# An attention-and-MLP block in a hand-written instruction order: another order for the same instructions

## The chip, the cores and the metric

The kernel runs on one core of one Trainium2 chip. The metric is the device time of one execution in microseconds. Three executions of the kernel before are known (median 170.43 us), and one execution was profiled.

## The reference

For 2048 tokens of 512 features, all in bf16, two blocks follow each other. The first is linear attention with 32 heads of 16 features, on a layer-normalised input:

```python
def _A_ref(x, wqkv, wo):
    ...
    phi = lambda t: jnp.where(t > 0, t + 1, jnp.exp(t)) + 1e-6
    pq, pk = phi(q), phi(k)
    kv = jnp.einsum("bhsd,bhse->bhde", pk, v)
    z = jnp.einsum("bhsd->bhd", pk)
    num = jnp.einsum("bhqd,bhde->bhqe", pq, kv)
    den = jnp.einsum("bhqd,bhd->bhq", pq, z)[..., None] + 1e-6
    o = num / den
...
h = x + _A_ref(_layernorm(x, axis=-1), A_wqkv, A_wo)
h2 = h + _B_ref(_layernorm(h, axis=-1), B_w1, B_w2)
```

The second block, `_B_ref`, is a ReLU MLP of 512 to 1792 to 512 features.

## The kernel before, in words

The tokens are 16 tiles of 128; four tiles make a chunk, so there are four chunks of 512 tokens. All weights and activations stay on chip. PSUM is one tile, `bk`, of eight banks of 512 fp32 columns, and each matmul group names its bank by number.

No scheduler orders the instructions. `ORDER` (line 18) is a long string of words, and the last lines of the kernel function go through it and call one small function for each word. The numbers behind a name are its arguments, so `K.8.0` is the keys of tile 8 in bank 0, `Q.2.3.2` the queries of chunk 2, feature block 3, in bank 2, and `f.1.1.0.7` seven of the fourteen products of tile 1 in bank 1.

```python
for word in ORDER.split():
    name, *idx = word.split(".")
    ops[name](*map(int, idx))
```

Each engine carries out its own words in the order of the string; semaphores between engines follow from the data (a reader waits for the writer, and a writer of a bank or buffer for its last reader). So an instruction that must wait also holds up everything behind it on its engine. The engines are PE (TensorE, matmuls), DVE (VectorE), ACT (ScalarE), POOL (GpSimd, masks only) and SP (SyncE), which issues every DMA: loads, stores and transposing DMAs.

The words, in the order in which the stages come (the lines are those of the kernel before):

| words | engine, line | what they do |
|---|---|---|
| lx, lk, lq, lv, lo, l1, l2 | SP, L201 and L204 | loads of x and of the weights for keys, queries, values, output, MLP |
| warmf, warm | PE, L221 and L215 | matmuls of zeros, whose results nobody reads |
| S, A | DVE, L237 and L238 | statistics of a tile of x, and their mean and variance |
| R | ACT, L243 and L244 | 1 / standard deviation of one or more tiles |
| N | DVE, L262 | the normalised tile, into `h_nat` |
| T and E | PE L281, ACT L291 | transpose of a normalised tile (tiles 0 to 3) and the copy into `lnT` |
| X | SP, L302 | the same by a transposing DMA (tiles 4 to 15) |
| K | PE, L310 | four matmuls of 512 columns: the keys of a tile |
| F, U, M, D or W | ACT L328 and L331, DVE L335, L338 or L343 | phi of the keys: exp, relu, min(exp, 1), the sum of both; W takes relu and sum in one step |
| G | PE, L362 | four matmuls that add the tile's normalised input times phi(keys) into banks 4 to 7 |
| za, zf, z, zc, zh | DVE, PE | the sum of phi(keys) over all tokens |
| Q, qF, qU, qM, qD or qW | PE L318, ACT, DVE | the queries of a chunk and phi of them, two feature blocks at a time |
| gA, kv, kx, m, mA | ACT, PE, DVE | the state: values' weights times G, masked by head, times wo, into `m_sb` |
| dn, dnl, dnx | PE L459, ACT L465, ACT L472 | the denominators of a chunk, and their reciprocals in two pieces of two tiles, into `wk_sb` (its weights are no longer needed) |
| dt | SP, L491 | transposing DMA of a tile's reciprocals into `rd`; for tiles 2 and 6 rt (PE) with rv (DVE) or re (ACT) does it |
| dm | DVE, L495 | phi(queries) times the reciprocals, into `pqs`, two feature blocks at a time |
| h, hD | PE L505, DVE L511 | four matmuls of `pqs` with the state, and the sum with x: the residual `h_nat` |
| s, a, r, n, x (or t and e) | DVE, ACT, DVE, SP L303 | the second normalisation and its transposes |
| p, pA or pD | PE L521, ACT L527 or DVE L532 | four matmuls with w1, and relu of two banks into `acts` |
| f, fo, fd | PE L541, DVE L549, SP L556 | fourteen matmuls with w2, the last sum, the store |

The words of different stages are interleaved. In the first 30 us the keys of a tile follow as soon as its transpose is there, and G follows phi of the keys. From about 39 us the state, the denominators and the queries of the later chunks come, h of chunk 0 follows at 50 us, and from 61 us p, h and f of different chunks alternate until the stores at the end.

Of the kernel before, what the change touches and what calls it, by code (L numbers as in the profile page):

```python
# [28 lines left out]
qU.0.2.2 lo.0.2 z.3.1.14 z.2.1.14 G.15 z.1.1.14 z.0.1.14 qD.0.2.2 zc gA.0.2 gA.2.2 Q.1.0.2 zh dn.0.1 Q.1.1.3
dnl.0 kv.2.7 lo.2.2 kv.1.7 kv.3.7 dnx.0.2.2 qF.1.0.2 kv.0.7 l2.3.4 dnx.0.0.2 Q.1.2.0 l1.2.2 rt.2.6 kx qM.1.0.2  # L30
Q.1.3.1 qF.1.2.2 m.0.4 m.1.5 rv.2 Q.3.1.7 qW.1.0.2 m.3.6 Q.2.3.2 dt.3 qM.1.2.2 mA.0.2 qW.1.2.2 dt.0 dt.1 m.2.5
Q.2.1.4 dn.1.0 mA.2.2 dm.0.0.2 Q.2.2.1 dm.0.2.2 dnl.1 dnx.1.2.2 h.3.6 dnx.1.0.2 h.1.5 rt.6.3 hD.3 qF.2.2.2 dt.7
s.3 re.6 h.0.0 dt.4 qU.2.2.2 hD.1 dt.5 a.3 hD.0 s.1 s.0 a.1 qM.2.2.2 a.0 Q.3.0.6 Q.2.0.3 n.3 h.2.5 n.0 dm.1.0.2
Q.3.3.1 x.3 dm.1.2.2 qF.3.0.2 hD.2 n.1 s.2 Q.3.2.0 qU.2.0.2 qF.2.0.2 h.5.2 h.6.3 a.2 qU.3.0.2 qM.2.0.2 h.4.7 n.2
qF.3.2.2 x.0 qD.2.0.2 t.2.5 qD.2.2.2 hD.4 x.1 hD.6 h.7.4 dn.2.6 hD.5 hD.7 e.2 dnl.2 qM.3.0.2 p.0.0.5 dnx.2.2.2
p.0.13.7 p.0.1.6 p.0.8.2 p.0.9.3 dnx.2.0.2 qD.3.0.2 s.4 l2.7.3 p.0.11.4 pA.0.0.2 dt.11 l2.0.3 dt.9 dt.10 r.0.4
qM.3.2.2 qW.3.2.2 s.6 dt.8 p.0.12.6 s.7 pD.0.12.2 p.0.3.1 p.0.2.0 pA.0.8.2 dn.3.2 p.0.5.7 dnl.3 p.0.4.6 a.7
dm.2.0.2 pA.0.2.2 dnx.3.0.2 dnx.3.2.2 dm.2.2.2 pD.0.4.2 h.9.0 h.8.5 p.0.6.6 p.0.7.7 dt.13 dt.12 s.5 dt.14
# [553 lines left out]
```

## Time and profile before

| what | us |
|---|---|
| median of three executions (lowest to highest) | 170.43 (170.37 to 170.6) |
| span of the profiled execution, first to last instruction | 168.8 |
| PE busy (855 instructions recorded) | 163.1 |
| DVE busy (205) | 104.4 |
| ACT busy (97) | 65.1 |
| data moved by DMA | 15.49 MB |

The span is shorter than the time of an execution, since what lies before the first and after the last instruction isn't in it. Times within the profile count from the start of the span. "Idle before" and the name behind an arrow say how long an engine had nothing to do before an instruction, and what ended that. PE's matmuls overlap at their ends, so its busy time says little about holes; some matmul records are missing from a trace (here 16 of 867). A transposing DMA has two times: how long SP needed to issue it, and from its issue to its landing.

### The profile page before, as it was taken

Reading aid. Unit: us, or ns where it says so; the run is one execution under the profiler, and the core shown is the slowest. Engines: PE = TensorE matmul, PEld = TensorE weight load, DVE = VectorE, ACT = ScalarE, POOL = GpSimd, SP = SyncE. Lnnn points to the kernel's source line nnn. Section 1 sums busy time; section 2 is a strip of 40 time slices with the busy share of each in tenths; the row PEclk is TensorE's granted clock in tenths of the full one; section 3 lists DMA queues with packets and bytes.
Section 4 is the critical chain, followed back from the end, with each engine's and each line's share of the span. In section 5 each row is a group of like instructions: output and inputs, shape, how many; then the busy total and the mean of one; then the engine's idle time right before and its main releaser. Section 6 shows DMA issues by size and latency. Waiting matters only on the chain.

```text
span 168.8 us, 2286 instructions
## 1 busy us (share of the span) xinstructions
PE 163.1 (97%) x855; PEld 78.0 (46%) x871; DVE 104.4 (62%) x205; ACT 65.1 (39%) x97; POOL 4.8 (3%) x21
## 2 busy tenths in 40 slices
PE   7989999999999999999999999999999999999993
PEld 5344344445644454444444444444444444444553
DVE  3899998997668999699819879215102432050251
ACT  3698775875879947432000003004320420400000
POOL 7400000000000000000000000000000000000000
PEclk9999999999999999999999999999999999999999
DMA  4975575689533353534130015500320000002023
GB/s 112 352 245 97 97 66 124 176 270 378 174 64 65 77 138 87 134 62 95 37 62 0 31 31 122 126 4 0 62 93 0 31 0 4 0 0 93 0 65 94
DMA packets 30491, 15.49 MB, mean 92 GB/s; under 512 B 23184, under 2 KB 29328, under 8 KB 30480
## 3 DMA queue, kind: packets, MB, share of 16 engines
q1 hardware_dynamic: 30480, 15.34, 35.5%
q8 instruction: 7, 0.11, 0.3%
q14 instruction: 4, 0.03, 0.1%
HBM read 7.86 MB, written 2.10 MB: 59 GB/s over the span
## 4 chain that ended last, share of the span: by engine, by line
PE 85%; DVE 7%; DMA 4%; issue 1%; SPq 0%
PE bk L541 29%; PE bk L521 28%; PE bk L505 8%; PE bk L318 8%; PE bk L362 6%; PE bk L310 4%; DVE st L237 3%; DMA x_nat<-in_A_x_dram 2%; DMA lnT<-h_nat 2%; DVE h_nat L262 2%; PE bk L459 1%; DVE eb L335 1%; PE bk L403 1%; PE bk L415 1%; SPq L201 0%
## 5 line engine op out<-in xcount | busy, mean ns | idle before, releaser
L541 PE MATMUL bk<-w_sb,at 128*128 128x512 bf16 (+2 forms) x247 | 50.1, 355 | 0.3
L521 PE MATMUL bk<-lnT,w_sb 128*128 128x512 bf16 x219 | 50.0, 379 | 0.3
L527 ACT ACTIVATE at<-bk 128x1024 bf16<-128x1024 f32 x14 | 14.2, 1023 | 57.4 <-PE bk L521 57.4
L541 PEld LDWEIGHTS <-at 128*128 128x128 bf16 x252 | 23.6, 98 | 25.4 <-ACT at L527 0.3
L549 DVE SCALAR_TENSOR_TENSOR gT<-bk,rstd,h_nat 128x512 bf16<-128x512 f32 (+2 forms) x18 | 12.2, 689 | 35.7 <-PE bk L541 35.6
L521 PEld LDWEIGHTS <-w_sb 128*128 128x128 bf16 x224 | 21.8, 98 | 25.8
L532 DVE TENSOR_SCALAR at<-bk 128x1024 bf16<-128x1024 f32 x14 | 17.1, 1218 | 12.8 <-PE bk L521 12.6
L328 ACT ACTIVATE eb<-bk 128x1024 bf16<-128x1024 f32 (+1 forms) x18 | 16.6, 928 | 6.6 <-PE bk L310 4.8
L310 PE MATMUL bk<-wk_sb,lnT 128*128 128x512 bf16 x63 | 15.3, 380 | 0.4 <-ACT lnT L291 0.3
L505 PE MATMUL bk<-m_sb,pqs 128*128 128x512 bf16 x63 | 15.4, 380 | 0.1
L318 PE MATMUL bk<-lnT,wq_sb 128*128 128x512 bf16 x61 | 15.1, 379 | 0.1
L362 PE MATMUL bk<-at,h_nat 128*128 128x512 bf16 x55 | 13.5, 379 | 0.1
L331 ACT ACTIVATE rb<-bk 128x1024 bf16<-128x1024 f32 (+1 forms) x14 | 12.5, 904 | 0.3 <-PE bk L310 0.3
L511 DVE TENSOR_TENSOR h_nat<-bk,x_nat 128x512 bf16<-128x512 f32 x16 | 10.5, 680 | 2.9 <-PE bk L505 2.9
L237 DVE BATCH_NORM_STATS2 st<-x_nat 128x6 f32<-128x512 bf16 x16 | 10.8, 680 | 2.4 <-DMA x_nat<-in_A_x_dram 2.4
L239 DVE BATCH_NORM_STATS2 st<-h_nat 128x6 f32<-128x512 bf16 x16 | 10.7, 683 | 0.1
L310 PEld LDWEIGHTS <-lnT 128*128 128x128 bf16 x64 | 6.0, 98 | 8.4 <-ACT lnT L291 1.0
L362 PEld LDWEIGHTS <-h_nat 128*128 128x128 bf16 x64 | 6.2, 98 | 7.4 <-issue 0.2
L505 PEld LDWEIGHTS <-pqs 128*128 128x128 bf16 x64 | 5.9, 98 | 7.9 <-DVE pqs L495 1.8
L318 PEld LDWEIGHTS <-wq_sb 128*128 128x128 bf16 x64 | 5.9, 98 | 6.4
L472 ACT ACTIVATE wk_sb<-ld 128x1024 bf16<-128x1024 f32 x8 | 8.1, 1050 | 0.1
L335 DVE TENSOR_SCALAR eb<-eb 128x1024 bf16<-128x1024 bf16 (+1 forms) x18 | 6.8, 383 | 0.9 <-ACT eb L328 0.9
(63 smaller groups left out, 93.5 us busy)
## 6 DMA issues: line engine op xcount, KB each, us to landing
out_dram<-gT SPq DMA_DIRECT2D x15, 128.0 KB, 1.9
w_sb<-in_B_w_dram SPq DMA_DIRECT2D x2, 896.0 KB, 9.8
x_nat<-in_A_x_dram SPq DMA_DIRECT2D x2, 512.0 KB, 6.3
w_sb<-in_B_w_dram SPq DMA_DIRECT2D x2, 512.0 KB, 9.5
x_nat<-in_A_x_dram SPq DMA_DIRECT2D x3, 256.0 KB, 4.6
w_sb<-in_B_w_dram SPq DMA_DIRECT2D x2, 384.0 KB, 3.5
wk_sb<-in_A_wqkv_dram SPq DMA_DIRECT2D x2, 256.0 KB, 4.3
wq_sb<-in_A_wqkv_dram SPq DMA_DIRECT2D x2, 256.0 KB, 4.9
```

What stands on the lines that cost most here:

```text
L237: op_S = lambda t: nc.vector.bn_stats(out=st[:, t, :], in_=x_nat[:, t, :])
L310: nc.tensor.matmul(bk[:, b, :], lhsT=lnT[c][:, kd, j * P : (j + 1) * P], rhs=wk_sb[:, kd, :], start=(kd == 0), stop=(kd == KD - 1),)
L318: nc.tensor.matmul(bk[:, b, :], lhsT=wq_sb[:, kd, j * P : (j + 1) * P], rhs=lnT[c][:, kd, :], start=(kd == 0), stop=(kd == KD - 1),)
L328: nc.scalar.activation(out=buf(eb, kind, i, n), in_=bank(at_bank[kind, i], n), func=ACT.Exp)
L331: nc.scalar.activation(out=buf(rb, kind, i, n), in_=bank(at_bank[kind, i], n), func=ACT.Relu)
L362: nc.tensor.matmul(bk[:, KD + kd, :], lhsT=ln_nat[:, t, kd * P : (kd + 1) * P], rhs=pk(t)[:, 0, :], start=(t == 0), stop=(t == NT - 1),)
L505: nc.tensor.matmul(bk[:, b, :], lhsT=pqs[:, (c * KD + jb) % NQ, j * P : (j + 1) * P], rhs=m_sb[:, jb, :], start=(jb == 0), stop=(jb == KD ...
L521: nc.tensor.matmul(bk[:, b, cols], lhsT=w1_sb[:, kd, f * P : (f + 1) * P], rhs=lnT[c][:, kd, cols], start=(kd == 0), stop=(kd == KD - 1),)
L527: nc.scalar.activation(out=acts[c % 2][:, f : f + n, :], in_=bank(at_bank["p", c, f], n), func=ACT.Relu)
L532: nc.vector.tensor_scalar(out=acts[c % 2][:, f : f + n, :], in0=bank(at_bank["p", c, f], n), scalar1=0.0, scalar2=None, op0=ALU.max,)
L541: nc.tensor.matmul(bk[:, b, 0 : w * P], lhsT=acts[c % 2][:, f, j * P : (j + 1) * P], rhs=w2_sb[:, f, k * P : (k + w) * P], start=(f == 0), ...
L549: nc.vector.scalar_tensor_tensor(out=o_t[:, t % NO, cols], in0=bk[:, at_bank["f", t, k], 0 : w * P], scalar=rstd2[:, t : t + 1], in1=h_nat ...
```

## The change

Only the string `ORDER` changes, and it becomes two lines shorter, so that each later line number is less by two. The instructions are the same in kind, number and size; their order on the engines and some bank numbers differ. The first lines show the kind of edit:

```diff
-const lx.0.1 lx.1.1 warmf.4.3 warm.1.3 S.0 table A.0 R.0.1 S.1 lx.2.2 lk.0.2 warm.1.3 N.0 A.1 S.2 R.1.1 lk.2.2
-lx.4.2 A.2 T.0.7 E.0 warm.1.3 S.3 R.2.1 K.0.1.0.2 lx.6.2 A.3 R.3.1 K.0.1.2.2 N.1 T.1.5 F.0.1 E.1 N.2 N.3 T.3.2
...
+lx.0.1 lx.1.1 lx.2.2 lk.0.2 lk.2.2 lx.4.2 lx.6.2 lx.8.4 lx.12.4 lq.0.2 const warmf.4.2 warm.1.5 S.0 A.0 table R.0.1
+S.1 N.0 A.1 S.2 A.2 T.0.3 R.1.1 E.0 R.2.1 S.3 A.3 N.1 N.2 R.3.1 N.3 warm.1.7 warm.1.0 K.0.3.0.2 K.0.3.2.2 T.1.1 E.1
...
```

What differs, from the front to the end:

- The first ten loads stand at the head of the string; SP's own order of them is as it was. The first transposes write separate banks (3, 1, 4, 7), where two of them shared bank 5. Tile 1's keys come in one piece ahead of those of tiles 3 and 2, where they came in two halves around tile 3's. E.1 and E.3 go ahead of F.0 on ACT, and E.2 behind U.0.
- On DVE the statistics S of tiles 9 and 8 go behind N.7 and N.6, and A.6 goes ahead of N.4. In the tiles that follow, phi of the keys often takes U before F, tile 13 comes ahead of 12 in S, and tiles 9 and 8 or 12 and 13 change places here and there. K.13 follows K.12 directly, where G.9 stood between.
- On SP the load lq.2.2 (before: after X.10) and lv.0.2 (before: after X.14) go ahead of X.12; l2.7.3 (before: after the x of chunk 0) and l2.0.3 (before: after dt.11) go ahead of dt.3.
- In the state: the two pieces of the first reciprocals, dnx.0.2 and dnx.0.0, follow each other on ACT; rt.2 and the products m stand in other places between the queries; for chunk 3, dnx.3.0 stands ahead of pA.0.2 on ACT, where it stood behind it.
- In the MLP: p, h and f take other orders among the tiles, h.9 comes later, the stores of a chunk go in another order, and tile 15's three pieces of 256, 128 and 128 columns come one after the other at the end, where one of 128 stood earlier.

Three places follow as the built programs have them, row by row (line, instruction, what it writes and reads, size, and how often in a row). The first is DVE, from the statistics of tile 7 to those of tile 8 (BN_STATS is S, BN_AGGR is A, TENSOR_SCALAR into `h_nat` is N, the other two are M and D). Before:

```order
L237 BN_STATS st<-x_nat 128x6
L262 TENSOR_SCALAR h_nat<-x_nat,mv,rstd 128x512
L338 TENSOR_TENSOR pk_lo<-rb,eb 128x512
L335 TENSOR_SCALAR eb<-eb 128x512
L238 BN_AGGR mv<-st 128x2 x2
L338 TENSOR_TENSOR at_94<-rb,eb 128x512
L237 BN_STATS st<-x_nat 128x6
L262 TENSOR_SCALAR h_nat<-x_nat,mv,rstd 128x512 x2
L237 BN_STATS st<-x_nat 128x6
```

And now, at the same place:

```order
L235 BN_STATS st<-x_nat 128x6
L236 BN_AGGR mv<-st 128x2
L260 TENSOR_SCALAR h_nat<-x_nat,mv,rstd 128x512
L336 TENSOR_TENSOR pk_lo<-rb,eb 128x512
L236 BN_AGGR mv<-st 128x2
L333 TENSOR_SCALAR eb<-eb 128x512
L336 TENSOR_TENSOR at_94<-rb,eb 128x512
L260 TENSOR_SCALAR h_nat<-x_nat,mv,rstd 128x512 x2
L235 BN_STATS st<-x_nat 128x6 x2
```

One of the two BN_AGGR moved ahead of N.4, and the BN_STATS of tile 9 moved behind the pair of normalisations N.7 and N.6.

The second place is ACT around the first reciprocals (gT is the state's first part, `ld` the logarithm of the denominators, `wk_sb` their reciprocals, `eb` the exp of a query pair, `m_sb` the state). Before:

```order
L395 ACTIVATE gT<-bk 128x1024 x2
L465 ACTIVATE ld<-bk,eps_74 128x128
L472 ACTIVATE wk_sb<-ld 128x1024
L328 ACTIVATE eb<-bk 128x1024
L472 ACTIVATE wk_sb<-ld 128x1024
L328 ACTIVATE eb<-bk 128x1024
L418 ACTIVATE m_sb<-bk 128x1024 x2
```

And now:

```order
L393 ACTIVATE gT<-bk 128x1024 x2
L463 ACTIVATE ld<-bk,eps_74 128x128
L470 ACTIVATE wk_sb<-ld 128x1024 x2
L326 ACTIVATE eb<-bk 128x1024 x2
L416 ACTIVATE m_sb<-bk 128x1024 x2
```

The exp of a query pair that stood between the two reciprocals now stands behind both.

The third place is SP from the last big loads on (`w_sb` is w1 or w2, `rd<-wk_sb` is dt, `lnT_81<-hn` is x of chunk 0). Before:

```order
L204 DMA w_sb<-in_B_w_dram 128x4x512
L204 DMA w_sb<-in_B_w_dram 128x2x1792
L491 DMA_TRANSPOSE rd<-wk_sb 128x4x128 x6
L303 DMA_TRANSPOSE lnT_81<-hn 128x4x128 x3
L204 DMA w_sb<-in_B_w_dram 128x3x512
L491 DMA_TRANSPOSE rd<-wk_sb 128x4x128
L204 DMA w_sb<-in_B_w_dram 128x3x512
L491 DMA_TRANSPOSE rd<-wk_sb 128x4x128 x7
```

And now:

```order
L202 DMA w_sb<-in_B_w_dram 128x4x512
L202 DMA w_sb<-in_B_w_dram 128x2x1792
L202 DMA w_sb<-in_B_w_dram 128x3x512 x2
L489 DMA_TRANSPOSE rd<-wk_sb 128x4x128 x6
L301 DMA_TRANSPOSE lnT_81<-hn 128x4x128 x3
L489 DMA_TRANSPOSE rd<-wk_sb 128x4x128 x8
```

The two loads of 3 x 512 columns moved from among the transposes of chunks 0 and 2 to the place ahead of all dt.

More of the change, by code (lines that the diff above doesn't have):

```diff
@@ L29 @@
[L29 to L38, printed above, removed]
@@ new lines @@
+Q.1.1.3 dnl.0 dnx.0.2.2 dnx.0.0.2 qF.1.0.2 rt.2.5 kx rv.2 qM.1.0.2 qW.1.0.2 Q.1.2.0 Q.1.3.1 m.3.6 m.0.4 m.1.5 Q.3.1.7
+qF.1.2.2 Q.2.3.2 dt.3 qM.1.2.2 qW.1.2.2 mA.0.2 dt.0 dt.1 m.2.5 Q.2.1.4 dn.1.0 mA.2.2 Q.2.2.1 dm.0.0.2 dm.0.2.2 h.3.5
+hD.3 s.3 dnl.1 dnx.1.2.2 rt.6.3 h.1.0 h.0.5 hD.1 dnx.1.0.2 dt.7 re.6 qU.2.2.2 qF.2.2.2 dt.4 dt.5 Q.3.0.6 Q.2.0.3 h.2.2
+Q.3.2.0 Q.3.3.1 a.3 hD.0 n.3 s.0 qM.2.2.2 s.1 a.0 a.1 n.0 dm.1.0.2 dm.1.2.2 qU.2.0.2 qF.2.0.2 qF.3.0.2 qU.3.0.2
+qF.3.2.2 hD.2 n.1 s.2 qM.2.0.2 a.2 n.2 h.5.3 h.4.2 h.6.6 t.2.5 h.7.4 x.3 x.0 x.1 qD.2.0.2 qD.2.2.2 dn.2.7 qM.3.2.2
@@ new lines @@
+qM.3.0.2 qW.3.2.2 hD.4 qD.3.0.2 hD.6 hD.7 hD.5 e.2 dnl.2 dnx.2.2.2 r.0.4 dnx.2.0.2 dt.11 dt.9 dt.8 dt.10 p.0.0.5
+p.0.13.7 p.0.8.0 dn.3.2 p.0.9.1 p.0.1.6 p.0.11.4 dnl.3 pA.0.8.2 pA.0.0.2 p.0.2.0 p.0.3.1 p.0.4.5 p.0.12.6 dnx.3.0.2
+pA.0.2.2 s.6 s.4 s.7 s.5 dm.2.2.2 a.7 dm.2.0.2 pD.0.12.2 p.0.6.0 p.0.10.3 p.0.7.1 a.5 pD.0.6.2 dnx.3.2.2 pA.0.10.2
+p.0.5.6 h.9.4 h.11.3 h.10.7 dt.14 dt.12 dt.15 dt.13 n.5 pD.0.4.2 n.7 hD.11 a.6 n.6 hD.9 s.11 dm.3.0.2 a.4 dm.3.2.2
+h.8.0 a.11 n.4 n.11 s.9 hD.8 s.8 f.0.5.0.7 f.2.2.0.7 h.12.6 h.15.4 h.14.3 f.0.5.7.7 f.1.0.0.7 h.13.1 x.4 hD.15 x.6 x.5
```

42 lines of the change are left out of this document (20 added, 22 removed).

## The prediction

> **What bounds the kernel now.** First the page: the span, and the chain that ended last by engine.
>
> ```profile
> span 168.8 us, 2286 instructions
> PE 85%; DVE 7%; DMA 4%; issue 1%; SPq 0%
> ```
>
> TensorE (PE) carries 85% of the chain. The rest is a head that waits for the first inputs, and a tail. The same chain in order of time (start, length, what) says where PE takes over, what a matmul costs, and where PE ends.
>
> ```profile
> 17.65 3.40 DMA lnT<-h_nat
> 21.10 1.04 PE bk L310 x4
> 129.81 10.14 PE bk L521 x47
> 166.18 0.35 DVE gT L549
> ```
>
> From 21.10 us to 166.1 us the chain lies on PE. A matmul of 512 columns takes 10.14 / 47 = 0.216 us. The last store's add starts at 166.18 and the span ends at 168.8, so the tail is 2.6 us. The matmuls are the same in number and size after the change. So only PE's idle time can change: I look for it by comparing where a row of the PE timeline starts with where the one before it must have ended (its start plus its count times 0.216). The ends that the profile shows overlap, so they don't serve.
>
> ```profile
> 12.13 1.02 PE L362 MATMUL bk<-pk_lo,h_nat 128*128 128x512 bf16 x4
> 19.94 1.03 PE L362 MATMUL bk<-at,h_nat 128*128 128x512 bf16 x4
> 21.10 1.04 PE L310 MATMUL bk<-wk_sb,lnT 128*128 128x512 bf16 x4
> 24.56 1.03 PE L310 MATMUL bk<-wk_sb,lnT 128*128 128x512 bf16 x3
> 49.54 0.81 PE L318 MATMUL bk<-lnT,wq_sb 128*128 128x512 bf16 x3
> 50.25 2.07 PE L505 MATMUL bk<-m_sb,pqs 128*128 128x512 bf16 x8
> 52.16 0.39 PE L281 MATMUL bk<-ident,wk_sb 128*128 128x128 bf16 x4
> 61.24 0.55 PE L459 MATMUL bk<-zhd,pqT 128*128 128x8 bf16 x16
> 61.64 1.67 PE L521 MATMUL bk<-lnT,w_sb 128*128 128x512 bf16 x7
> 70.24 1.46 PE L521 MATMUL bk<-lnT,w_sb 128*128 128x512 bf16 x6
> 71.62 2.07 PE L505 MATMUL bk<-m_sb,pqs 128*128 128x512 bf16 x8
> 73.53 0.81 PE L521 MATMUL bk<-lnT,w_sb 128*128 128x512 bf16 x3
> ```
>
> Three holes stand there. **K.8** (tile 8's keys) starts at 21.10 where G.4 ended at 19.94 + 0.86 = 20.80: 0.30 us. **h.3**, the first product of chunk 0 with the state: 49.54 + 0.65 = 50.19 against 50.25, and its eight matmuls take 52.16 - 50.25 = 1.91 instead of 1.73: 0.24 us in all. **h.9**: 70.24 + 1.30 = 71.54 against 71.62, and 73.53 - 71.62 = 1.91 instead of 1.73: 0.26 us. All three wait for transposing DMAs. The first shows it in the chain; for the others it is VectorE (DVE) that waits, before the multiplications (dm) that feed h:
>
> ```profile
> 49.50 1.29 DVE L495 TENSOR_TENSOR pqs<-pqT,rd 128x1024 bf16<-128x1024 bf16 x2 [1.02 <-DMA rd<-wk_sb]
> 70.88 1.29 DVE L495 TENSOR_TENSOR pqs<-pqT,rd 128x1024 bf16<-128x1024 bf16 x2 [1.61 <-DMA rd<-wk_sb]
> ```
>
> Up to G.0 at 12.13 PE has much idle time, but there it waits for D.0, the last DVE step on tile 0's keys. So the head counts by D.0 alone.
>
> **The change part by part.**
>
> *Head.* These DVE rows are S.7, N.4, D.0 and the pair A.7, A.6 that follows:
>
> ```profile
> 10.74 0.68 DVE L237 BATCH_NORM_STATS2 st<-x_nat 128x6 f32<-128x512 bf16 x1
> 11.35 0.40 DVE L262 TENSOR_SCALAR h_nat<-x_nat,mv,rstd 128x512 bf16<-128x512 bf16 x1
> 11.66 0.42 DVE L338 TENSOR_TENSOR pk_lo<-rb,eb 128x512 bf16<-128x512 bf16 x1
> 12.20 0.24 DVE L238 BATCH_NORM_AGGREGATE mv<-st 128x2 f32<-128x6 f32 x2
> ```
>
> A.6 now stands ahead of N.4 and so ahead of D.0. One of the pair is worth at most 0.12, half of its 0.24, and at least nothing; as DVE has no gap here I take **+0.10**. G.0 moves from 12.13 to 12.23. The other head moves end before that. K.1 in one piece ahead of K.3 costs nothing if its copy E.1 is early, and it now stands ahead of F.0. On ScalarE (ACT) E.2 goes behind U.0:
>
> ```profile
> 10.20 0.58 ACT L291 ACTIVATE lnT<-bk 128x512 bf16<-128x512 bf16 x1
> 10.68 0.59 ACT L331 ACTIVATE rb<-bk 128x512 bf16<-128x512 f32 x1
> ```
>
> They change places, so E.2 ends where U.0 ended, at 11.27, and K.2's four matmuls run from 11.32 to 12.18, just ahead of the new G.0. That is cover by a few hundredths; whatever it falls short, G.0 pays. U.0 starts half a microsecond sooner, which D.0 can't use, as it stands behind N.4.
>
> *K.8.* X.8 was issued at 17.65 and landed 3.40 later. SyncE's queue (SP) issues ten such transposes from 10.85 on, with gaps; one gap is before X.7, which waits for N.7, which stood behind S.9 on DVE:
>
> ```profile
> 12.73 0.69 DVE L237 BATCH_NORM_STATS2 st<-x_nat 128x6 f32<-128x512 bf16 x1
> 13.33 0.72 DVE L262 TENSOR_SCALAR h_nat<-x_nat,mv,rstd 128x512 bf16<-128x512 bf16 x2
> 10.85 14.66 SPq L302 DMA_TRANSPOSE lnT<-h_nat  x10
> 13.75 1.19 SPq L302 DMA_TRANSPOSE lnT<-h_nat  x1
> ```
>
> N.7 and N.6 now go ahead of S.9, so they start up to 13.33 - 12.73 = 0.60 sooner. X.7 is third in line: X.5 and X.4 occupy SP from 10.85 for two steps of 1.27 (3.81 / 3, the row of three transposes further down), so X.7 can start at 13.4, 0.35 sooner than 13.75, and X.8, three places on, near 17.35. Even with the same 3.40 it lands at 20.75, and K.8 is due at 20.80 + 0.10 = 20.90. The hole goes: **-0.30**. A later landing leaves part of it. What is late next is below.
>
> *K.12 and K.13.* Two 256 KB loads (the second half of the query weights, the first of the value weights) now stand ahead of X.12 and X.13 on SP, and K.13 directly behind K.12, ahead of G.9. K.12 moves with PE from 24.56 to about 24.38, and K.13 is due 0.86 later, at 25.24. These rows are, in this order: X.13's issue, its time from issue to landing, that of the twelve transposes of this line together, and that of the three loads of this size that SP issued between 25 and 31 us.
>
> ```profile
> 21.11 1.19 SPq L302 DMA_TRANSPOSE lnT<-h_nat  x1
> DMA to landing us min/median/max: 4.1/4.1/4.1
> DMA to landing us min/median/max: 2.4/2.5/4.1
> DMA to landing us min/median/max: 2.9/3.0/3.1
> ```
>
> X.8 at 17.35, two load issues, X.12: X.13 is issued near 21.1 as before. With 2.5 it lands at 23.6 and nothing waits; with the 4.1 that it took, at 25.2, on the very point. With the loads in its way as well it is later by up to 1.2: the second load, issued at 19.2, lands 3.0 later, at 22.2, and if X.12 (issued at 19.8, due to land at 22.3) must follow it whole, it lands a step of 1.27 after that, and X.13 after X.12. So the bounds are 0 and 1.2. I take **+0.10**, near the low end, since the median of the twelve is 2.5. By the Trainium skill ("DMA: Bandwidth & Descriptors", Queues, rings and completion order), SP's DMAs share one row of rings, and each DMA engine consumes its ring in order; so the loads' bytes would go first. By that rule this term is the first rival's 0.66 whenever X.13 is as late as before. Whether a transpose waits for the loads ahead of it no row above shows.
>
> K.12 writes a bank that F.8 must have read. U.8 and F.8 change places, with R.10 now ahead of both: 0 to 0.1, I take **+0.03**. Q.2.3 waits in the same way for a DVE step (W of a query pair) that now comes behind rv.2: **+0.05**, between 0 and 0.1.
>
> *h.3.* dt.3, dt.0, dt.1 are transposes of the reciprocals, which ACT writes in two pieces (L472), with F of a query pair between them:
>
> ```profile
> 42.35 1.06 ACT L472 ACTIVATE wk_sb<-ld 128x1024 bf16<-128x1024 f32 x1
> 43.31 1.01 ACT L328 ACTIVATE eb<-bk 128x1024 bf16<-128x1024 f32 x1
> 44.21 1.05 ACT L472 ACTIVATE wk_sb<-ld 128x1024 bf16<-128x1024 f32 x1
> ```
>
> Now the two follow each other, so the second ends 44.21 - 43.31 = 0.90 sooner, and dt.0 and dt.1, which wait for it, can be issued sooner by half of that or more (dt.3 is ahead of them on SP). dm waited 1.02 and PE lost only 0.24, so a quarter of a microsecond is enough: **-0.24**. Against it: the last two w2 loads, 768 KB, now stand in front of dt.3. But one of 256 KB that stood there is gone ahead, another no longer delays X.15 before them, and SP comes to all of them sooner. I let this end between -0.24 and +0.24, as much the other way.
>
> *h.9.* Between the transposes of chunk 2 stood one of those loads, and another shortly before:
>
> ```profile
> 63.30 1.69 SPq L491 DMA_TRANSPOSE rd<-wk_sb  x1
> 65.04 0.58 SPq L204 DMA_DIRECT2D w_sb<-in_B_w_dram  x1
> 65.73 3.81 SPq L491 DMA_TRANSPOSE rd<-wk_sb  x3
> ```
>
> Without it the three at 65.73 go at least 65.73 - 65.04 = 0.69 sooner, and h.9 now stands later in PE's order: **-0.26**. What is late next here is ACT: dnx.3.0 (1.05) now stands ahead of the evacuation pA.0.2 (about 1.02, as the row of L328 for the same size). dnx.3.0 overwrites what dt.8 reads, so it waits for dt.8's landing, and p.0.6 waits behind both. p.0.0 started at 61.64 and by the terms so far comes 0.26 sooner, at 61.38; ten products of four matmuls (8.64) and the 16 small ones of dn.3 (0.40, as 61.24 to 61.64) stand ahead of p.0.6: due 70.42. dt.8 is the third of four, the first issued at 63.30 - 0.26; with two steps of 1.27, or one of 1.69 and one of 1.27, it is issued at 65.6 to 66.0, lands 2.5 later, and 2.0 later pA.0.2 has ended: 70.1 to 70.5. Cost 0 to 0.1, I take **+0.10**.
>
> *The rest* (order of p and f, banks, stores, the split of tile 15) changes none of PE's work. Each of these groups writes a bank whose emptying was put before other groups of four or seven matmuls, 0.9 to 1.5 us, and that is the cover; where it is gone, an evacuation of about 1.0 (L328's row, for two banks) shows as a hole. The last add and store have the size they had: 0.
>
> Sum: 0.10 - 0.30 + 0.10 + 0.03 + 0.05 - 0.24 - 0.26 + 0.10 = -0.42. The sum is against the profiled execution: 168.8 becomes 168.4. The median of the runs, 170.43, stands 1.6 above that span; I keep that distance: **170.0 us**.
>
> **The rivals.** About 0.2% (0.34 us) is what a measurement of this kernel can tell from no change; the forecast lies just beyond it.
>
> *The loads delay the transposes.* X.12's and X.13's bytes come after the loads' bytes, half of the 1.2 above since part of them is through by then, and X.13 again takes 4.1: it lands at 25.9 and K.13 waits 0.66 in place of 0.10. The sum is +0.14: 170.55. For it: X.13 took 4.1 with only other transposes around. Against: most transposes take 2.5, and 1.6 us of cover is there. Chance 0.24, of which 0.03 for nearly the whole 1.2 and an end on the slower side. The Trainium skill's rule on the rings, above, is this rival carried through.
>
> *A gain stays out.* The transposes before h.3 or h.9 are late for another reason than their place in the order (they took up to 4.1 elsewhere), and 0.25 is not won: 170.25. Chance 0.15, within 0.2%.
>
> *ACT behind dt.8.* If dt.8, issued at 66.0, takes 3.4 rather than 2.5, dnx.3.0 and pA.0.2 end at 71.4 and PE waits 1.0 at p.0.6: -0.42 - 0.10 + 1.0 = +0.48, 170.9. It decides for slower from a landing of 3.3 us on. For it: the 3.40 of X.8. Against: the load that stood among these transposes is gone. Chance 0.13.
>
> **How the numbers follow.** The forecast has 0.48; it is the likeliest. The range goes down to 169.7, where the new waits (0.28 without the head) don't come, and up to 170.75: it leaves out the slower ends and little else. Faster 0.48, within 0.2% 0.36 (0.21 and 0.15), slower 0.16 (0.13 and 0.03).
>
> **What would show it.** In the profile after: K.8 without a hole near 20.9; G.0 at 12.2; K.13 at 25.2 to 25.4; the DMA waits of L495 on DVE (2.6 us together) mostly gone and L505 running eight matmuls in 1.73; p.0.6 near 70.4; the last add near 165.75. I am wrong if a wait of PE above 0.3 us stands anywhere after 21 us, at K.13 or p.0.6 above all, or if the last add isn't sooner than 166.18.

## The result, and the profile after

The changed kernel took 171.72 us (median of four, 171.15 to 171.79), the kernel before 170.4 in the same series: a ratio of 1.0071, 95% interval 1.0049 to 1.0093. It is slower by about 1.3 us where 0.42 less was forecast, and above the range. Two later series with twelve executions each gave 1.0015 (0.9997 to 1.0032) and 1.0032 (1.0010 to 1.0053): the sign is the same, the size varies, and the first of the two can't be told from no change. Four executions of later series, of 248 to 608 us, are left out of the ratios.

The page after, first the span and the chain:

```profile
span 169.4 us, 2300 instructions
PE 83%; DVE 6%; DMA 5%; ACT 2%; issue 1%; SPq 0%; DVEq 0%
```

The span grew by 0.6 us, and DMA has 5% of the chain where it had 4%. The chain in order of time shows at which place:

```profile
19.91 4.96 DMA lnT<-h_nat
24.92 1.90 PE bk L308 x8
...
49.88 0.88 PE bk L316 x4
50.76 0.86 PE bk L503 x4
...
64.96 9.52 PE bk L519 x44
74.47 3.45 PE bk L503 x16
```

The first row is X.12, which took 4.96 us to land; K.12 and K.13 (24.92) follow it. The load lv.0.2 is the row just ahead of X.12 on SP; it landed 4.85 us after its issue, at 24.21, and X.12 0.66 after that, at 24.87:

```profile
19.36 0.46 SPq L202 DMA_DIRECT2D wv_sb<-in_A_wqkv_dram  x1
```

The other rows answer to the holes of before: h.3 starts at 50.76, where the queries end (49.88 + 0.88), and h.9 at 74.47, where 44 matmuls of the groups p (9.52 / 44 = 0.216 each) end without a gap, p.0.6 among them. The PE timeline around K.8 and K.12:

```profile
20.08 1.03 PE L360 MATMUL bk<-at,h_nat 128*128 128x512 bf16 x4
20.94 1.03 PE L308 MATMUL bk<-wk_sb,lnT 128*128 128x512 bf16 x4
21.80 2.75 PE L360 MATMUL bk<-at,h_nat 128*128 128x512 bf16 x12
24.92 1.90 PE L308 MATMUL bk<-wk_sb,lnT 128*128 128x512 bf16 x8 [0.36 <-DMA lnT<-h_nat]
```

K.8 (20.94) follows G.4 without a hole. Before K.12 the twelve matmuls end at 21.80 + 2.59 = 24.39, and K.12 starts at 24.92: 0.53 us are lost. On DVE the wait for the reciprocals is 1.5 us in place of 2.6:

```profile
L493 DVE TENSOR_TENSOR pqs<-pqT,rd 128x1024 bf16<-128x1024 bf16 x8 | 5.3, 678 | 1.5 <-DMA rd<-wk_sb 1.5
```

So up to the last matmul the changed kernel is a little ahead: its last add starts at 166.09, against 166.18. But its span ends 0.6 later. These rows of the timeline are the last stores on SP (start, duration) and the last add on DVE:

```profile
163.78 0.33 SPq L554 DMA_DIRECT2D out_dram<-gT  x1
164.44 0.33 SPq L554 DMA_DIRECT2D out_dram<-gT  x1
165.04 1.50 SPq L554 DMA_DIRECT2D out_dram<-gT  x1
166.63 0.86 SPq L554 DMA_DIRECT2D out_dram<-gT  x2
166.09 0.35 DVE L547 SCALAR_TENSOR_TENSOR gT<-bk,rstd,h_nat 128x128 bf16<-128x128 f32 x1 [0.43 <-PE bk L539]
```

From the DMA view of 164.5 to 165.0 us, the fetch of instructions on queue q8 (packets, MB, share of 16 engines):

```profile
q8 instruction: 1, 0.02, 18.4%
```

The issue of the store of 256 columns takes 1.50 us instead of 0.33, and the two stores behind it start at 166.63 and 167.11; the last could have started at 166.44, when its add ended. In the same stretch one packet of 16 KB fetches PE's next instructions; it took 0.184 x 16 x 0.5 = 1.47 us, from 164.70 to 166.17. From the start of the last add to the end it takes 3.35 us, not 2.66. I call this the tail.

The profile before has the same kind of row earlier: an issue of 1.03 us at 163.52, and then two of 0.33 with nothing in front of them; its packet (DMA view of 162.5 to 163.0 us) ran from 162.86 for 0.166 x 16 x 0.5 = 1.33 us:

```profile
163.52 1.03 SPq L556 DMA_DIRECT2D out_dram<-gT  x1
165.91 0.33 SPq L556 DMA_DIRECT2D out_dram<-gT  x1
166.56 0.33 SPq L556 DMA_DIRECT2D out_dram<-gT  x1
```

```profile
q8 instruction: 1, 0.02, 16.6%
```

In all twenty profiles of this case, altered kernels included, one issue beside this last packet is longer than the others, and it ends 0.2 to 0.4 us after the packet does (here 166.54 against 166.17). In the profile before that is over long before the last add.

### The profile page after: what moved, and what is told of

Its sections match the earlier page's. It is cut to its first block, busy times and chain, and to the rows that moved or that the text cites. A ratio compares the mean times of both kernels' runs of the same rounds, so it can differ in the third digit from the quotient of the medians.

```text
span 169.4 us, 2300 instructions
## 1 busy us (share of the span) xinstructions
PE 163.2 (96%) x871; PEld 77.7 (46%) x871; DVE 104.6 (62%) x205; ACT 64.6 (38%) x97; POOL 4.8 (3%) x21
## 4 chain that ended last, share of the span: by engine, by line
PE 83%; DVE 6%; DMA 5%; ACT 2%; issue 1%; SPq 0%; DVEq 0%
PE bk L539 29%; PE bk L519 29%; PE bk L316 8%; PE bk L503 8%; PE bk L360 4%; PE bk L308 3%; DMA lnT<-h_nat 3%; DVE st L235 3%; DMA x_nat<-in_A_x_dram 2%; DVE h_nat L260 1%; PE bk L457 1%; ACT rb L329 1%; ACT eb L326 1%; DVE at L336 1%; DVE mv L236 1%
## 5 line engine op out<-in xcount | busy, mean ns | idle before, releaser
L519 PE MATMUL bk<-lnT,w_sb 128*128 128x512 bf16 x224 | 49.5, 379 | 0.0
L316 PE MATMUL bk<-lnT,wq_sb 128*128 128x512 bf16 x64 | 15.6, 379 | 0.0
L241 ACT ACTIVATE rstd<-mv,eps 128x2 f32<-128x2 f32 (+2 forms) x14 | 4.1, 296 | 22.9 <-DVE mv L238 16.9
```

The source lines that it names most:

```text
L316: nc.tensor.matmul(bk[:, b, :], lhsT=wq_sb[:, kd, j * P : (j + 1) * P], rhs=lnT[c][:, kd, :], start=(kd == 0), stop=(kd == KD - 1),)
L519: nc.tensor.matmul(bk[:, b, cols], lhsT=w1_sb[:, kd, f * P : (f + 1) * P], rhs=lnT[c][:, kd, cols], start=(kd == 0), stop=(kd == KD - 1),)
```

## The experiments

The theory after the two profiles: the two loads delay X.12 (the first rival of the prediction, one transpose earlier than it said), and the fetch, whose place depends on the number of PE's instructions, holds up the last stores. The rivals: X.12 is late by the fetch near 22 us alone; the tail comes from the new order of the stores.

### The changed kernel again, and three first edits

No edit:

> The changed kernel once more, unaltered, as the mark for the others. Both theories expect 1.004 to 1.009 of the kernel before and, in the profile, the two losses seen once: a hole of about 0.5 us at K.12 near 24.9 and 3.3 us from the start of the last add to the end of the span, against 2.6 before.

Measured: 170.41 against 170.09, ratio 1.0015 (0.9997 to 1.0032), less than the 1.004 that both theories expected. The hole at K.12 was 0.31, the tail 3.03.

An earlier last piece:

```diff
-f.12.0.0.7 f.12.0.7.7 f.8.2.0.7
+f.12.0.0.7 f.15.4.0.14.3.1 f.12.0.7.7 f.8.2.0.7
...
-fd.12 fd.10 fo.8
+fo.15.3.1 fd.12 fd.10 fd.15.3.1 fo.8
...
-fo.15.2.1 fd.15.2.1 f.15.4.0.14.3.1 fo.15.3.1 fd.15.3.1
+fo.15.2.1 fd.15.2.1
```

> The changed kernel with the last 128 columns of tile 15 computed earlier, ahead of the second half of tile 12 (in the kernel before such a piece also stood earlier), and their add and store earlier with them. Theory 1 (the block of PE's instructions, 16 KB, that is fetched at 164.70 in the changed kernel and at 162.86 in the kernel before holds up SP's stores): with 14 small matmuls gone from the end, the fetch comes near 163, the tail falls from 3.3 to 2.6 us, and the time by about 0.7. Theory 2 (the order of the big stores: three of 128 KB come in the last microseconds, and the fetch does nothing): the big stores stay where they are, so the tail falls by 0.2 at most.

Measured: 1.0070 (1.0043 to 1.0097), slower than the unaltered kernel beside it (171.26 against 170.41 us), with a tail of 2.98: the numbers of both theories missed. The fetch came at 163.57, in the midst of the big stores. The DVE timeline shows what that did:

```profile
164.25 0.75 DVE L547 SCALAR_TENSOR_TENSOR gT<-bk,rstd,h_nat 128x512 bf16<-128x512 f32 x1 [2.01 <-PE bk L539]
166.55 1.40 DVE L547 SCALAR_TENSOR_TENSOR gT<-bk,rstd,h_nat 128x512 bf16<-128x512 f32 x3 [1.55 <-DMA out_dram<-gT]
```

An add waited 1.55 us for the landing of an earlier store, whose buffer it overwrites. A store delayed there costs more than one at the end. The edit changed order and fetch together and so can't tell the theories apart.

The loads back:

```diff
-lq.2.2 lv.0.2 X.12 X.13
+X.12 X.13
...
-X.10 K.12.0
+X.10 lq.2.2 K.12.0
...
-X.15 X.14
+X.15 X.14 lv.0.2
```

> The changed kernel with the two loads lq.2.2 and lv.0.2 behind X.10 and X.14 again, as in the kernel before. Theory 1 (the loads' bytes go ahead of X.12's and push them into the instruction fetch at 22.3): X.12 lands within 3 us, the hole of 0.53 us at K.12 goes, and the last add comes about 0.5 sooner, the time by 0.4 to 0.5. Theory 2 (the fetch alone delays X.12, as it delayed X.13 in the kernel before): X.12 or X.13 still takes 4 us or more and a hole of 0.3 or more stays.

Measured: 1.0031 (1.0008 to 1.0053), so the 0.4 to 0.5 us of theory 1 didn't come (170.65 against 170.41). The PE timeline at K.12, and at h.3 (of the four matmuls at 48.94 one record is missing, as 16 of the 871 are in this trace, and in the first profile of the kernel before):

```profile
21.73 2.54 PE L360 MATMUL bk<-at,h_nat 128*128 128x512 bf16 x11
24.10 1.89 PE L308 MATMUL bk<-wk_sb,lnT 128*128 128x512 bf16 x7
...
48.94 1.02 PE L316 MATMUL bk<-lnT,wq_sb 128*128 128x512 bf16 x3
50.04 1.21 PE L503 MATMUL bk<-m_sb,pqs 128*128 128x512 bf16 x4
```

K.12 starts as the eleven matmuls end (21.73 + 2.38 = 24.11): the hole is gone, so the loads made it. X.12 still took 4.2 us, with a fetch at 21.0 while it was under way (2.4 in the kernel before, where the fetch came later and X.13 took 4.1). That fits a delay by the fetch too; without the loads it doesn't reach K.12. What I hadn't expected: h.3 starts at 50.04, 0.24 after the queries' end (48.94 + 0.86), and its four matmuls take 1.21 instead of 1.03: 0.4 us. With the two loads later on SP, the w2 loads behind them are later too, and dt.3 lands 5.2 us after its issue (3.2 in the changed kernel). What the change paid at K.12 it had won back at h.3.

The late piece in the kernel before:

```diff
-f.13.4.0.7 f.15.0.0.14.3.1 f.14.5.7.7
+f.13.4.0.7 f.14.5.7.7
...
-fd.10 fd.11 fo.15.3.1 fo.8
+fd.10 fd.11 fo.8
...
-fd.12 fo.13 fd.15.3.1 fo.15.0.2
+fd.12 fo.13 fo.15.0.2
...
-fo.15.2.1 fd.15.2.1
+fo.15.2.1 fd.15.2.1 f.15.3.0.14.3.1 fo.15.3.1 fd.15.3.1
```

> The kernel before with tile 15's pieces of 256, 128 and 128 columns one after the other at the end, as in the changed kernel; all else as before. Theory 1 (fetch): the fetch moves from 162.9 to 164.6 or so, the tail grows from 2.6 to about 3.3, the time by 0.5 to 0.8. Theory 2 (order of the big stores, which is untouched here): the tail grows by 0.2 at most, 1.000 to 1.002.

Measured: 1.0005 (0.9985 to 1.0025). The fetch did move to 164.77, but the tail was 2.70: a fetch among the last stores doesn't always cost something. Its row in the DMA view (164.5 to 165.0 us):

```profile
q8 instruction: 1, 0.02, 10.9%
```

This packet took 0.109 x 16 x 0.5 = 0.87 us, not 1.47, and was over at 165.65, before the last add. The long issue beside it (0.50 us) ended at 166.02, and the last store started right behind its add, which ended at 166.27.

### Loads and fetch taken apart

> The changed kernel a third time, unaltered, as the mark for the three below and to see how far its distance from the kernel before moves from one series to the next (so far 1.0071 and 1.0015). Expected: 1.001 to 1.007, a hole of 0.3 to 0.5 us at K.12, a tail of 3.0 to 3.4 us.

Measured: 170.94 against 170.13, 1.0032 (1.0010 to 1.0053); hole at K.12 0.14, less than expected, and tail 3.08.

```diff
-lq.2.2 lv.0.2 X.12 X.13
+X.12 X.13 lq.2.2 lv.0.2
```

> The changed kernel with lq.2.2 and lv.0.2 behind X.13 in place of ahead of X.12: SP waits there for N.11 anyway, from 22.4 to 23.4. Theory 1 (the loads' bytes go ahead of X.12's): X.12 lands no later than 23.5 and the hole at K.12 falls from 0.3 to 0.5 us to less than 0.1, while h.3 stays without a hole, as SP is free just as early; the time is 0.3 to 0.5 below the unaltered changed kernel. Rival (the place of the loads doesn't matter, the instruction fetch near 21 to 22 delays X.12 or X.13 by itself): a hole of 0.2 or more stays at K.12 or K.13. Second rival: X.11 now follows the loads and lands late, and the hole moves to K.11.

Measured: 170.50, 1.0031 (1.0008 to 1.0053). The hole was gone and h.3 had none, as the theory says; X.12 landed at 23.0. From G.0 to the last matmul it took 153.12, the shortest so far. But the tail was 3.08. The median lay 0.44 below the unaltered kernel's, while the two ratios (1.0031 and 1.0032) are the same: a gain in time is not shown.

```diff
-p.2.5.5 p.2.4.4 p.2.8.6 p.3.1.3 p.3.8.0
+p.2.5.5.0.2 p.2.5.5.1.2 p.2.4.4.0.2 p.2.4.4.1.2 p.2.8.6.0.2 p.2.8.6.1.2
+p.3.1.3.0.2 p.3.1.3.1.2 p.3.8.0.0.2 p.3.8.0.1.2
```

> The changed kernel with five groups p (2.5, 2.4, 2.8, 3.1, 3.8) each computed in two halves of 256 columns: 20 matmuls more, the same columns, so PE takes no longer, but its instruction numbers run 20 matmuls ahead and the last fetch comes 20 matmuls earlier. Theory 1 (the last fetch, 16 KB at 164.70 in the first profile, holds up the stores around it): the fetch comes near 162.2, between the stores of 161.6 and 163.8; no store's issue takes over 0.6 from 163.7 on, the tail is 2.6 to 2.8 in place of 3.0 to 3.4, and the time 0.3 to 0.6 below the unaltered changed kernel. Theory 2 (the order of the stores): the tail stays at 3.0 to 3.4, the time the same within 0.1.

Measured: 170.07, 0.9991 (0.9974 to 1.0007), which is 0.87 below the unaltered kernel beside it, with the same order of stores. The DMA view of 160.0 to 160.5 us, then from the timeline the store of 256 columns and the last add:

```profile
q8 instruction: 1, 0.02, 12.2%
```

```profile
164.65 0.33 SPq L554 DMA_DIRECT2D out_dram<-gT  x1
165.71 0.35 DVE L547 SCALAR_TENSOR_TENSOR gT<-bk,rstd,h_nat 128x128 bf16<-128x128 f32 x1 [0.43 <-PE bk L539]
```

The fetch came at 160.43, earlier than I had expected; the store that took 1.50 us takes 0.33 like every one after 163; and the span ended at 168.36, 2.65 after the last add began. The executions also scatter less: 169.5 to 170.7, against 169.8 to 171.8.

> Both edits together. If theory 1 holds in both, the gains add: 0.6 to 1.1 below the unaltered changed kernel, and 0.2 to 0.8 below the kernel before (0.995 to 0.999). If only the loads matter it is as the run with the loads alone, if only the fetch matters, as the run with the split groups.

Measured: 170.01, 0.9998 (0.9982 to 1.0013); no hole at K.12, tail 2.67. The gains didn't add in the time: with the fetch away, the loads are worth less than this measurement can tell. That the tail is the fetch's stands (two of two with it moved, at 2.65 and 2.67, and the same order of stores).

### Were the two holes of the kernel before there to win?

> The kernel before, unaltered, for a second profile of it. Theory A (the prediction's: the holes before h.3 and h.9, 0.24 and 0.26 us, belong to the order of the instructions): they are there again, with DVE's waits of 1.0 and 1.6 us at L495, and from the start of G.0 to the start of the last matmul it takes 153.7 to 153.9 us as in the first profile. Theory B (they came of that one execution): at least one of them is absent, and the stretch takes about 153.4, as in the run with the late piece, which had neither.

> The kernel before, unaltered, for a third profile. Theory A: both holes, 153.7 to 153.9 us from G.0 to the last matmul. Theory B: at least one absent, about 153.4. Under both the hole at K.8 of 0.3 to 0.4 us is there.

Measured: 170.03 and 169.79, with spans of 168.3 and 168.1 where the first profile had 168.8. The PE timeline of the first at K.8, h.3 and h.9:

```profile
19.86 1.03 PE L362 MATMUL bk<-at,h_nat 128*128 128x512 bf16 x4
21.08 1.04 PE L310 MATMUL bk<-wk_sb,lnT 128*128 128x512 bf16 x4 [0.20 <-DMA lnT<-h_nat]
...
49.31 1.02 PE L318 MATMUL bk<-lnT,wq_sb 128*128 128x512 bf16 x4
50.17 1.89 PE L505 MATMUL bk<-m_sb,pqs 128*128 128x512 bf16 x8
51.90 0.39 PE L281 MATMUL bk<-ident,wk_sb 128*128 128x128 bf16 x4
...
69.55 1.89 PE L521 MATMUL bk<-lnT,w_sb 128*128 128x512 bf16 x8
71.28 1.89 PE L505 MATMUL bk<-m_sb,pqs 128*128 128x512 bf16 x8
73.00 2.32 PE L521 MATMUL bk<-lnT,w_sb 128*128 128x512 bf16 x10
```

K.8 lost 21.08 - 20.72 = 0.36 (0.32 in the other). But h.3 starts at 50.17, where the queries end (49.31 + 0.86), and runs its eight matmuls in 1.73; h.9 likewise (69.55 + 1.73 = 71.28; 73.00 - 71.28 = 1.72). Both holes are absent in both, and the stretch from G.0 to the last matmul takes 153.33 and 153.34, not 153.79. Theory B holds: I had priced two holes of one execution.

The two edits that I had given 0.50 us, alone in the kernel before:

```diff
-dnx.0.2.2 qF.1.0.2 kv.0.7 l2.3.4 dnx.0.0.2
+dnx.0.2.2 dnx.0.0.2 qF.1.0.2 kv.0.7 l2.3.4
...
-Q.1.2.0 l1.2.2 rt.2.6
+Q.1.2.0 l1.2.2 l2.7.3 l2.0.3 rt.2.6
...
-l2.7.3
...
-l2.0.3
```

> The kernel before with the two edits alone that the prediction gave 0.50 us: the first reciprocals dnx.0.2 and dnx.0.0 one after the other on ACT, and the loads l2.7.3 and l2.0.3 ahead of dt.3. Theory A (the prediction's): neither hole, 0.3 to 0.5 us less, 0.997 to 0.998 of the kernel before. Theory B (the holes came of one execution): h.9 has no hole, but there is nothing to gain on most executions: 0.999 to 1.001. Theory C (the two loads now queue ahead of dt.3, and without lq.2.2 and lv.0.2 gone from SP's queue before them they make it late, as in the run with the loads back, whose h.3 had a hole of 0.40): a hole of 0.2 to 0.5 at h.3, 1.000 to 1.003.

Measured: 170.95, 1.0053 (1.0039 to 1.0068), slower by more than any theory had said. The PE timeline at h.3, and dt.3's time from issue to landing:

```profile
49.56 1.02 PE L318 MATMUL bk<-lnT,wq_sb 128*128 128x512 bf16 x4
51.01 2.07 PE L505 MATMUL bk<-m_sb,pqs 128*128 128x512 bf16 x8 [0.43 <-DVE pqs L495]
```

```profile
DMA to landing us min/median/max: 5.2/5.2/5.2
```

h.3 waits 51.01 - 50.42 = 0.59, and its matmuls lose another 0.16; 0.25 more is lost at the query group before it (at 47 us). It is theory C, with a larger price: dt.3 stands behind 768 KB of loads and lands 5.2 us after its issue, at 48.56 and 0.5 after the last of these loads (48.06), as it lands 0.5 after its last load in all three profiles of the kernel before (46.33 after 45.83 in the first). So these edits lose by themselves, and the early loads lq.2.2 and lv.0.2 are what made them harmless in the change, as the run with the loads back says too (0.4 lost at h.3).

### Where the slower executions lose

> The changed kernel, unaltered, for one more profile: its executions scatter from 169.75 to 171.8 and those profiled so far lie in the faster half. Theory 1 (the last fetch, which holds up the stores for as long as its packet takes, makes the scatter): in a profile above 171 us the excess stands in the tail, 3.5 us or more, with a packet of 1.5 us or more. Theory 2 (the arrival of the x loads at the front): the excess stands before G.0, with lx.2.2 or lx.4.2 landing 0.5 or more later than 5.5 and 7.8. Theory 3 (the loads ahead of X.12): it stands between G.0 and the last matmul, over 153.6.

> As the run before: one more profile of the changed kernel, read in the same three stretches (to G.0, to the last matmul, tail), with the same three theories.

> As the two before: one more profile of the changed kernel, read in the same three stretches, with the same three theories.

Measured: 170.77, 170.94 and 170.89. None of them exceeded 171 us, so the theories could only be read from smaller differences. All unaltered profiles in three stretches (G.0's start from the timeline; G.0 to the start of the last matmul; the tail; the packet from the DMA view):

| kernel, us | G.0 | G.0 to last matmul | tail | span | last packet |
|---|---|---|---|---|---|
| before, first profile | 12.13 | 153.79 | 2.66 | 168.8 | 1.32 |
| before, second | 12.06 | 153.33 | 2.67 | 168.3 | 0.97 |
| before, third | 11.81 | 153.34 | 2.68 | 168.1 | 1.10 |
| changed, first profile | 12.24 | 153.60 | 3.35 | 169.4 | 1.47 |
| changed, second | 11.76 | 153.33 | 3.03 | 168.4 | 1.36 |
| changed, third | 12.09 | 153.22 | 3.08 | 168.6 | 1.27 |
| changed, fourth (170.77) | 12.02 | 153.41 | 3.29 | 169.0 | 1.42 |
| changed, fifth (170.94) | 11.93 | 153.31 | 3.66 | 169.1 | 1.70 |
| changed, sixth (170.89) | 12.87 | 153.27 | 2.78 | 169.2 | 0.94 |

In the changed kernel the tail grows with the packet, though not strictly (1.36 has 3.03, 1.27 has 3.08): the shortest packet has the shortest tail, the longest the longest. The run with the late piece fits too (0.87 and 2.70). The fifth profile in rows, the fetch (164.0 to 164.5 us; 0.212 x 16 x 0.5 = 1.70 us), then a store's issue and the last add, 3.66 before the end:

```profile
q8 instruction: 1, 0.02, 21.2%
```

```profile
164.44 1.80 SPq L554 DMA_DIRECT2D out_dram<-gT  x1
165.49 0.35 DVE L547 SCALAR_TENSOR_TENSOR gT<-bk,rstd,h_nat 128x128 bf16<-128x128 f32 x1 [0.43 <-PE bk L539]
```

The sixth is late for another reason: the load lx.4.2 landed at 8.88 us instead of 7.3 to 8.1, and all of the front is later with it. So theories 1 and 2 both make scatter, the loads (theory 3) little. The means of six against three: +0.15 at G.0, -0.13 between, +0.53 in the tail. Against the second and third profile of the kernel before alone, the middle is level: the 0.34 that K.8 lost there is spent at K.12 (0.28 on average) and in a new hole of up to 0.1 near 15.5 us. The profiles come from several chips; the median of the kernel before differs by 0.15 us among them (169.98 to 170.13).

### A version without the causes

First the two edits together with A.6 behind D.0 again:

```diff
-N.5 S.7 A.6 N.4 D.0.1 A.7
+N.5 S.7 N.4 D.0.1 A.7 A.6
```

> The changed kernel with the two loads behind X.13 and the five split groups, and in addition A.6 behind D.0 on DVE again, as in the kernel before. Expected by the stretches of the profiles so far: G.0 0.08 us sooner after X.5's issue (1.28 in place of 1.36), no hole at K.12, tail 2.65: 0.1 below the run with both edits, 0.998 to 0.9995 of the kernel before. Rival (A.6 isn't on the path, R.6 or N.6 behind it is): no difference.

Measured: 170.06, 0.9999 (0.9987 to 1.0011). G.0 still came 1.36 after X.5's issue (1.27 to 1.30 in the kernel before), so A.6's return alone wins nothing; and this execution shows a hole at K.11, the second rival of the run with the loads in the gap:

```profile
25.66 1.03 PE L360 MATMUL bk<-at,h_nat 128*128 128x512 bf16 x4
26.98 1.25 PE L308 MATMUL bk<-wk_sb,lnT 128*128 128x512 bf16 x5 [0.29 <-DMA lnT<-h_nat]
```

X.11, behind both loads, landed at 26.93, and K.11 lost 26.98 - 26.52 = 0.46.

Then one load behind X.13, the other behind X.10, and E.2 ahead of U.0 (the split groups and A.6 stay):

```diff
-lq.2.2 lv.0.2 X.12 X.13
+X.12 X.13 lq.2.2
...
-X.10 K.12.0
+X.10 lv.0.2 K.12.0
...
-R.4.2 U.0.1 E.2
+R.4.2 E.2 U.0.1
```

> The changed kernel with the five split groups, lq.2.2 behind X.13 and lv.0.2 behind X.10 (no load ahead of a transpose that is due at once), A.6 behind D.0 and E.2 ahead of U.0 again. Expected: no hole at K.12 and none at K.11, K.2's matmuls 0.5 sooner, so that G.0 comes 1.28 after X.5's issue instead of 1.36, about 153.1 from G.0 to the last matmul, tail 2.65: 0.998 to 0.9995 of the kernel before. Rival (h.3 is late again, since lv.0.2 is one place later): a hole of 0.2 to 0.4 at h.3, 1.000 to 1.002.

Measured: 169.70 against 169.99, 0.9985 (0.9971 to 1.0000). No hole at K.12 or K.11, 0.12 at h.3, tail 2.67. But G.0 came 1.41 after X.5's issue, so the return of A.6 and E.2 together wins nothing at the front either. The last two runs:

> The last run's best kernel, unaltered, once more: 0.9975 to 1.0 of the kernel before. Its profile showed that K.2's matmuls still began only at 11.24, where U.0 had read bank 3, which K.0 and K.2 share.

> The same kernel with K.0 in bank 0 in place of 3, so that K.2, in bank 3, no longer waits for U.0's reading of K.0. Theory (the shared bank, not the place of E.2 or A.6, delayed K.2 and with it G.0): K.2 starts within 0.1 of the end of E.2, G.0 comes 1.26 to 1.30 after X.5's issue in place of 1.36 to 1.43, and the time is 0.1 below that of the run beside it. Rival: G.0 stays at 1.36 or more.

```diff
-K.0.3.0.2 K.0.3.2.2
+K.0.0.0.2 K.0.0.2.2
```

Measured: 0.9985 (0.9971 to 0.9998) for the first, as in the series before it: 0.25 us less than the kernel before, with an interval that ends just below 1, and less than the changed kernel by more. For K.0 in bank 0: 0.9985 (0.9971 to 1.0000). The timeline at K.2 and G.0, first of the changed kernel itself (first profile; the second row is D.0 on DVE), then of the last kernel with the shared bank (its first series), then of the one with the other bank:

```profile
11.37 1.04 PE L308 MATMUL bk<-wk_sb,lnT 128*128 128x512 bf16 x4 [0.46 <-ACT lnT L289]
11.73 0.42 DVE L336 TENSOR_TENSOR pk_lo<-rb,eb 128x512 bf16<-128x512 bf16 x1
12.24 1.03 PE L360 MATMUL bk<-pk_lo,h_nat 128*128 128x512 bf16 x4
```

```profile
11.24 1.02 PE L308 MATMUL bk<-wk_sb,lnT 128*128 128x512 bf16 x4 [0.46 <-ACT rb L329]
```

```profile
11.18 1.04 PE L308 MATMUL bk<-wk_sb,lnT 128*128 128x512 bf16 x4 [0.76 <-ACT lnT L289]
12.47 0.81 PE L360 MATMUL bk<-pk_lo,h_nat 128*128 128x512 bf16 x3 [0.25 <-DVE pk_lo L336]
```

In the changed kernel K.2 waits for E.2, which stands behind U.0 on ACT, and G.0 follows K.2 without a hole (11.37 + 0.86 = 12.23); it is so in all twelve profiles with E.2 in that place. D.0, which ended at 12.15, isn't what ends last, and that is why A.6's return won nothing. With E.2 ahead of U.0, K.2 waits for U.0 (rb), which must have read K.0 out of the bank that both share. Only with the other bank as well does K.2 wait for E.2 at its old place, and G.0 (12.47) for D.0 again, 1.28 after X.5's issue. So E.2's place made the front's 0.1 us in the change, and the shared bank kept it when E.2 went back. What the bank alone, or A.6 alone, would cost no run shows. Won back, the 0.1 us doesn't show in the time.

## Why the prediction was wrong

Between the two first profiles, which the sum was about, two terms account for the miss: K.12's wait (0.53 where 0.13 was said for it and the bank) and the tail (0.68 where 0 was said). With the waits at p.0.6 and Q.2.3 that didn't come (0.15), they turn -0.42 into +0.51; the spans differ by +0.60, and a new hole of 0.07 near 15.5 us is most of the rest. The prediction's own sign of being wrong, a wait of PE above 0.3 us after 21 us, was there at K.12. Its other one was not, as the last add came at 166.09. Over several profiles a third term fails, that of h.3 and h.9.

- **Head, +0.10.** The size was right (G.0 at 12.24 against 12.23 said; 1.35 to 1.43 after X.5's issue against 1.27 to 1.30), but the term stood on the wrong wait. It is not D.0 behind A.6 that ends last but K.2 behind E.2, which the prediction had as cover by a few hundredths and put at nothing. E.2 did end at 11.32, near the 11.27 said; K.2 started 0.05 after it and ended at 12.23. So the right size was in part luck. The bank that K.0 and K.2 now share I had passed over.
- **K.8, -0.30.** Right. The hole is in every profile of the kernel before (0.30, 0.36, 0.32) and in none of the changed one. X.8 is issued about 0.3 sooner against G.0, as said, but it also lands after 2.4 to 2.5 us instead of 3.4 to 3.5 in all six, which I hadn't said; why is open.
- **K.12 and K.13, +0.13.** The first failed step, and the first rival came true one transpose earlier: I looked at X.13, and X.12 was late. It stands behind both loads, is issued 0.6 us later after X.8 (2.45 against 1.81 with the loads back) and lands after 4.6 to 5.0 us (3.9 to 4.3 in the runs without the loads ahead); the hole is 0.53 in the first profile, 0.14 to 0.33 in the others. The term was put near the low end of its bounds, and the bounds took 3.0 us for the second load: lv.0.2 took 4.4 to 4.85 in the six profiles, with a fetch of PE's instructions in its way, and X.12 landed 0.66 to 0.69 after it in each. What the fetch and the first load each add to lv.0.2's time is not separated. By the rule of the Trainium skill ("DMA: Bandwidth & Descriptors", Queues, rings and completion order) each DMA engine takes its ring in order. The trace agrees: transposes behind loads land after them, X.12 as said, and dt.3, where the w2 loads are late, after 5.2 us instead of 2.9 to 3.3 in the unaltered kernels.
- **h.3 and h.9, -0.50 together.** The step that failed most on the side of gains. Both holes stood in the rows, but in one execution; two further profiles have neither. The edits that were to remove them cost 0.9 us when made alone, since they put 768 KB ahead of dt.3. The prediction had named that risk, with 0.24, and taken the loads gone ahead as its cover; those were the cover indeed.
- **p.0.6, +0.10, and the other waits.** Not there: 44 matmuls run without a gap. The third rival didn't come: dt.8 landed 2.5 us after its issue. The second came true in its outcome, as the gain at h.3 and h.9 stays out against two of the three profiles of the kernel before, but for another reason than it gave: those two hadn't lost it.
- **"The last add and store have the size they had: 0."** The other failed step, and the largest term: +0.53 on average, 0.1 to 1.0. The size of the last store is the same, but the piece of 14 small matmuls that moved to the end brings PE's last fetch to 1.0 to 1.4 us ahead of the last add, where it was 3.3 to 3.5, and the last stores queue behind an issue that ends only after it. How the fetch holds the issue up is not shown. That the fetch is needed for it is shown (six profiles with split groups, all with a tail of 2.65 to 2.67 and the same order of stores). Whether the new order of the stores adds to it is not settled: in the kernel before, with the fetch as late and its own order, twelve executions gave a ratio of 1.0005 (0.9985 to 1.0025). The row of 1.03 us at 163.52 stood in the profile before; I had costed the order of the stores by PE's work alone, and not by SP's queue or by what else the DMA engines carry then.

By the stretches, the changed kernel should be 0.55 us behind the kernel before; the series say 0.32, 0.81 and 1.3. Why the first series lay so high stays open: three of its four executions, at 171.7 to 171.8, have no profile, and no later profile of the unaltered kernel was as long. The kernel before, too, was at its longest in that series (170.4, later 169.98 to 170.13), and which chip it ran on isn't on record. A longer tail is possible but not shown.

## What to carry to other kernels

A hole of a few tenths that hangs on a transfer is worth pricing only if a second profile has it too, since the same transfer of the same kernel landed up to 1.6 us apart here (lx.4.2, 7.3 to 8.9 us in the changed kernel). When loads or stores change places in a queue, name the next transfer behind each and what waits for it: a load that leaves one place delays another. And when the last microseconds are rearranged, look at SP's issues and at q8 there, since a fetch moves with the number of PE's instructions ahead of it.

## What the runs showed of the hardware

- A fetch of PE's instructions is one packet of 16 KB and took 0.87 to 1.76 us at the end of the kernel. Beside it one of SP's DMA issues took up to 2.35 us instead of 0.33 (1.50 and 1.80 in the rows above, 2.35 in the run with the earlier last piece), and stores of 128 KB that were under way landed after up to 4.1 us instead of 1.8 (3.3 and 3.6 in the first profile). The Trainium skill ("Runtime: NRT & Kernel Launch", Instruction fetch mechanics) has the blocks of 16 KiB and calls their cost "mostly hidden". For PE that agrees, as no hole of PE follows directly from one of its fetches; for the DMAs around it the runs differ, and in the tail it cost up to 1.0 us.
- Twenty matmuls more at no PE time (groups of 512 columns in two halves of 256) moved the last fetch from about 164.5 to 160.4 us and took 0.87 us off the median.
- The load lx.4.2, issued at 3.2 us in all profiles, landed between 7.3 and 8.9 us, and G.0 started between 11.76 and 12.91, earliest and latest where this load was.
